# Moving the tiles of a four-layer fp32r kernel in SBUF: three unused pad tiles and a smaller DMA scratch

## The chip, the cores and the metric

The kernel runs on one core of one Trainium2 chip. The metric is the device time of one execution in microseconds (us), lower is better. Times of the kernel before: 1810.0 us, the median of three runs (1809.1 to 1810.69).

## What is computed

`x` holds 2048 positions of 640 features in fp32. Four layers follow one another, A, B, A, B, each `x = x + layer(layernorm(x))` (below, the layer inputs are normalised):

```python
# layer A: 32 heads of 20, each position attends to itself and to 7 earlier ones, 2 apart
q, k, v = split(x @ wqkv)                       # wqkv is 640 x 1920
attn = softmax(q . k[pos - 2*w] * 20**-0.5)     # w = 0..7, masked where pos - 2*w < 0
y = concat_heads(sum_w attn * v[pos - 2*w]) @ wo
# layer B: real part of a 2-D Fourier transform, as matrix products
a, b = x @ dft_hid_re.T, x @ dft_hid_im.T       # 640 x 640
y = dft_seq_re @ a - dft_seq_im @ b             # 2048 x 2048
```

## The kernel before

**Numbers in two parts.** TensorE works on fp32r operands. Every matrix is split into a high part and a low remainder, and each product is three matmuls, high·high, high·low and low·high (`PASSES`). A split tile has the shape `[128, 2, ...]`, with the parts side by side. Nearly all of TensorE's work is of that kind, 8798 matmuls in all, each with its own weight load.

**Layer A** (`layer_a`) goes over 32 units of work (a block of 512 positions and a group of four heads) in steps, and a plan written out in the code gives each step its phases on all engines. `qkv_mm` (L347, matmul at L357) makes the QKV projection of one of 4 position blocks, one of 4 head groups `q` and one of 4 sub-blocks `j`: 15 matmuls of 480 columns, with the transposed input in tile `s{j}` as weights (stationary) and the projection's split weights in tile `r1_{q}` as the moving operand. There are 64 such groups in each layer A. `tp` and the functions `pc_pe` and `pc_sub` transpose 128x128 blocks with the moving operand `ident` (L322) and subtract with the weights `nident` (L330). `wo_mm` (L504) is the output projection. VectorE and GpSimd do the attention itself in tiles `pr0` to `pr3` (L426, L434, L464, L479).

**Layer B** (`LayerB`) has three kinds of matmuls. `z_mm` (L903, matmul at L914) multiplies a normalised input block (`xn[c]`, tile `r1_{c}`, stationary, 128 columns `k`) with a split block of the sequence matrix (`ct[s]`, 512 columns, moving). There are 16 steps `s` of 15 matmuls for one column block: `s // 4` is `c`. The first column block is done inside the end of layer A, with `ct[s]` in tile `s3`, `s0`, `s2` in turn (four tiles in turn from step 12), the second by `run` (L1225) through `zpart` with `ct[s]` in `s3` for even `s` and `s0` for odd `s`. The five banks `m0, m1, xt, t0, t1` take the five `k` of each of the three passes.

The other six column blocks are made in three calls of `pair` (L1089) per layer, with Strassen's scheme of seven products. `product` (L1078, matmul at L1081) issues three matmuls of 512 columns for each of its banks: the weights are 128-column pieces of a tile `r1_c`, the moving operand a split block in `r1_2`, `r1_3`, `s0` or `s1`. A call of `pair` has three sections of eight rounds `i`:

- first, per round, `m5` (six matmuls, banks `m`), `m4` (six, banks `xt` and `t`) and `m7` (six, banks `t` and `pq`): 144 in all. `m4`'s weights lie in `r1_2` and `r1_3`; those of `m5` and `m7` in `r1_0` for rounds 0, 1, 4 and 5, in `r1_1` for the others (`x_slot` goes round a ring of eight places, four in each tile, two places a round).
- second, `m2` (six), `f1` (three), `f2` (three), `m1` (six), `f1` (three): 168 in all. `m1` and `m2` go by the same ring; the first `f1` has `r1_0` for rounds 0 to 3 and then `r1_1`; the others have `r1_2` and `r1_3`.
- third, `m3` (six), `f2` (three), `m6` (six): 120 in all. `m3` and `f2` have `r1_0` for rounds 0 to 3 and then `r1_1`; `m6` has `r1_1`. From round 3 on a twelve-matmul piece of `ymm` stands between the rounds, so that rounds 0 to 3 are one stretch of 60.

Counted over a call, 48 + 60 + 36 = 144 of the 432 matmuls take their weights from `r1_0`. Two layers with three calls make 864 of 2592.

`ymm` (L981, matmul at L992) is the hidden transform: for each of five `k`, twelve matmuls of 320 columns, whose moving operand is in turn `wr` (tile `r2a`) and `wi[k]` (tiles `pr0` to `pr3` and `zo3`), 16 output tiles in each layer.

**Order of the work.** Layer A is written out for all engines. In layer B only TensorE's order is (`tc.manual_schedule`); the order of the other engines and of the loads, which SP issues, is made by the planner of `tile.TileContext(nc, schedule_with_timeline_sim=True)`. The kernel's DMAs are issued from SP, eight of them from ScalarE, none from GpSimd.

**Where a tile lies.** `T` asks the pool for a tile by a tag. A tag gets its place at its first request, in order of the requests, as large as its largest tile and rounded up to 32 bytes per partition; later tiles of the tag use it again. Ahead of them lie the reserved scratch for DMA descriptors (16384 bytes at address 0 when nothing else is asked for) and four constants of 32 bytes. So `warm` begins at 16512. The places that matter, in bytes per partition, with the remainder of the address by 128:

```
warm   16512   0      r1_0  22784   0      pr1   65984  64     r1_3  147904  64
ident  16544  32      pr0   43264   0      r1_1  81344  64     zo2   168384  64
nident 17056  32      win   48384   0,64   r2a  101824  64     s0    185536  64
s3     17568  32      (5 buffers, in turn) r1_2 127424  64     zo0   216512  64
```

The other tiles of matmul operands (`pr2`, `pr3`, `zo1`, `zo3`, `ot`, `s1`, `s2`, `stg`, `xa`) have the remainder 64. The pieces of them that matmuls use begin at multiples of 128 bytes within their tile (480 x 4 = 1920, 320 x 4 = 1280, 128 x 4 = 512), so that a piece has its tile's remainder. The last tile ends at 229312.

Of the kernel before, what the change touches and what calls it, by code (L numbers as in the profile page):

```python
# [26 lines left out]
P = 128  # L27
# [47 lines left out]
def tile_layers(ctx: ExitStack, tc: tile.TileContext, x, wqkv, wo, cs, wre, wim, out):  # L75
    nc = tc.nc
# [9 lines left out]
    def nm(base):  # L86
        uid[0] += 1
        return f"{base}_{uid[0]}"

    def T(shape, tag, dt=F32, bufs=1, pool=None):  # L90
        return (pool or sb).tile(shape, dt, tag=tag, name=nm(tag), bufs=bufs)
# [4 lines left out]
    warm = T([P, 1], "warm")  # L96
    nc.vector.memset(warm, 0.0)
    nc.scalar.activation(warm, warm, AF.Exp)
    ident = T([P, P], "ident")
    make_identity(nc, ident)  # L100
    nident = T([P, P], "nident", F32R)
# [6 lines left out]
    mhalf = T([P, 4], "mhalf")  # L108
    nc.gpsimd.memset(mhalf, -0.5)
    mask = T([P, SLOTS], "mask")  # L110
    nc.gpsimd.memset(mask, 0.0)
    nc.gpsimd.memset(mask[0:2, 0:3], NEG)
    nc.gpsimd.memset(mask[0:1, 3:7], NEG)
# [74 lines left out]
    def load_x(src, j, tag="xa"):  # L188
        xt = T([P, D], tag, bufs={"xa": 2}.get(tag, 1))
        nc.sync.dma_start(xt, src[:, j, :])  # L190
        return xt
# [10 lines left out]
    def wq_load1(q, k):  # L202
        raw = wtile([P, 3 * F])
        nc.sync.dma_start(raw, wqkv[q][:, k, :])
        return raw
# [31 lines left out]
    def layer_a(li, stats, handoff, prev):  # L237
# [21 lines left out]
        def at(step, phase, fn, *args):  # L259
            plan.setdefault((step, phase), []).append((fn, args))  # L260
# [5 lines left out]
        def x_load(c, j, tag="xa"):  # L266
            xnT[(c, j)] = load_x(xin[c], j, tag)

        def x_stats(c, j, fast=False):
            if j == 0:  # L270
                stats[c] = Stats()
            stats[c].tile(j, xnT[(c, j)], fast)

        def x_fin(c, j):
            stats[c].finish(j, j + 1)

        def x_norm(c, j, fast=False):
            stats[c].apply(j, xnT[(c, j)], fast)

        def xt_pe(c, j, part, bank):  # L280
            if part == 0:
                xnT[(c, j, 1)] = T([P, 2, KD, P], f"s{j}", F32R)
            xnT[(c, j, "p", part)] = t_pe(xnT[(c, j)], part, bank)

        def xt_hi(c, j, part):
            t_hi(xnT[(c, j, 1)], part, xnT[(c, j, "p", part)])

        def xt_lo(c, j, part):
            t_lo(xnT[(c, j, 1)], part, xnT[(c, j, "p", part)])
# [236 lines left out]
        def wq_begin(q):  # L526
            wq[q] = T([P, 2, KD, 3 * F], f"r1_{q}", F32R)

        def wq_raw(q):
            if q < 3:  # L530
                if q == 1:
                    wq["raw"] = T([P, 2, KD, 3 * F], "r2a")
                nc.sync.dma_start(wq["raw"][:, q - 1], wqkv[q])
                for k in range(KD):
                    wq[(q, k)] = wq["raw"][:, q - 1, k]
                return
            for i, tag in enumerate(("zo2", "zo3", "ot")):
                k0, k1 = 2 * i, min(2 * i + 2, KD)
                raw = wq_load(q, k0, k1, tag)
                for k in range(k0, k1):  # L540
                    wq[(q, k)] = raw[:, k - k0]
# [64 lines left out]
        def prologue_first():  # L606
            wq_begin(0)
            for j, (k0, k1) in enumerate(((0, 3), (3, 5))):
                x_load(0, j, f"pr{j}")
                for k in range(k0, k1):  # L610
                    wq[(0, k)] = wq_load1(0, k)
            for j in range(2, NJ):
                x_load(0, j, f"pr{j}")
            for q in (1, 2, 3):
                wq_begin(q)
                wq_raw(q)
            w0 = wq[0]

            def whi(k, eng):
                (eng.tensor_copy if eng is nc.vector else eng.copy)(w0[:, 0, k], wq[(0, k)])  # L620

            def wlo(k, eng):
                eng.tensor_tensor(w0[:, 1, k], wq[(0, k)], w0[:, 0, k].bitcast(F32), op=ALU.subtract)

            def xt_all(j, bank):
                return [(xt_pe, (0, j, i, f"{bank}{i}")) for i in range(2)] + [
                    (f, (0, j, i)) for i in range(2) for f in (xt_hi, xt_lo)
                ]

            x_stats(0, 0, True)  # L630
            x_fin(0, 0)
            for k in range(3):
                whi(k, nc.scalar)
            wlo(0, nc.vector)
            x_norm(0, 0, True)
            wlo(1, nc.gpsimd)
            for i in range(2):
                xt_pe(0, 0, i, f"t{i}")
            for i in range(2):
                xt_hi(0, 0, i)  # L640
            x_stats(0, 1, True)
            wlo(2, nc.gpsimd)
            x_fin(0, 1)
            whi(3, nc.vector)
            whi(4, nc.vector)
            for i in range(2):
                xt_lo(0, 0, i)
            wlo(3, nc.vector)
            wlo(4, nc.vector)
            x_norm(0, 1, True)  # L650
            x_stats(0, 2, True)
            x_fin(0, 2)
            mid[0] = xt_all(1, "aux") + [(x_stats, (0, 3, True)), (x_fin, (0, 3)), (x_norm, (0, 2, True))]
            mid[1] = xt_all(2, "t") + [(x_norm, (0, 3, True)), (zero_rows, ())]
            mid[2] = xt_all(3, "aux")
            for i in range(KD):
                at(LEAD0[0] + 1 + i // 2, "misc", wq_split, 1, i)
                at(LEAD0[0] + 3 + i, "misc", wq_split, 2, i)
                at(LEAD0[0] + 5 + i, "misc", wq_split, 3, i)
# [31 lines left out]
        while len(gs) < NGRP:  # L691
            if st % 2 == 0 and len(tx) < NC * NJ:
                c, j = divmod(len(tx), NJ)
# [114 lines left out]
        with tc.manual_schedule(engines=ENGINES):  # L808
            if first:
                prologue_first()  # L810
            nc.vector.tensor_copy(mk, mask)
            for s in range(LEAD0[0], last + 1):
                for ph in PHASES:
                    for fn, args in plan.pop((s, ph), ()):
                        fn(*args)
            pc_pe(67)
            pc_hi(67)
            pc_lo(67, True)
            wo_mm(c, 2, None, 0, 2, 3)
            wo_mm(c, 3, ("pq", "aux0"))  # L820
            wo_add(c, 2)
            wo_stats(c, 2)
            wo_fin(c, 2, 3)
            if first:
                handoff.c_hl(14)
            handoff.ln_tail(c, 2, xr, nstats)
            wo_add(c, 3)
            handoff.ln_lo(c, 2)
            handoff.z_mm(14, None)
            wo_stats(c, 3)  # L830
            wo_fin(c, 3, 4)
            if first:
                handoff.c_hl(15)
            handoff.ln_tail(c, 3, xr, nstats)
            handoff.ln_lo(c, 3)
            handoff.z_mm(15, None)
# [478 lines left out]
```

## Time and profile before

| what | value |
|---|---|
| median of three runs | 1810.0 us (1809.1 to 1810.69) |
| span of the profiled execution, first to last instruction | 1804.2 us |
| mean granted TensorE clock over the span | 0.993 |
| TensorE matmul, busy | 1745.8 us (97%) |
| VectorE, busy | 1392.7 us (77%) |
| ScalarE, busy | 818.3 us (45%) |
| GpSimd, busy | 633.5 us (35%) |

For the profiled execution the profile gives the span alone and no device time of its own; the median of the runs is 5.8 us above that span. A row of the timeline has the start in us from the span's start, the length from the first start to the last end in us, the engine, the line, the operation, the tiles as `output<-inputs` without their buffer numbers (so `r` is any of `r1_0` to `r1_3`, and `s` any of `s0` to `s3`), the shape and the count of instructions that were merged into the row. The end of a matmul is modelled and overlaps the next one, so the pace of a run of matmuls is read from starts alone: start of a later row less start of an earlier one, divided by the matmuls between them. A row of the table by stretches has the stretch, its length, then busy time and count for PE (matmul), PEld (weight load), DVE (VectorE), ACT (ScalarE) and POOL (GpSimd), the granted TensorE clock as a share of full speed, the mean busy share of the DMA engines, and GB/s.

### The profile page before, as it was taken

To read this page: it belongs to the slowest core of one execution; us is meant where nothing else is said; L and a number is where in the kernel's file an instruction comes from. 1 tells how busy PE (TensorE), PEld (TensorE's weight loads), DVE (VectorE), ACT (ScalarE), POOL (GpSimd) and SP (SyncE) were. 2 spreads that over 40 slices of the span, in tenths; PEclk is the share of its full clock that TensorE was granted. 3 is DMA by queue.
4 is the path that set the end of the run, shared out by engine and by line. 5 is a ranking of instruction groups with operands and counts; after the bars stand their busy time and mean duration, and the time that the engine had idled before them with its cause. 6 is when DMAs were issued, how large, how long until landed. Compare 5 with 4: busy or idle time off the path is not lost.

```text
span 1804.2 us, 26493 instructions
## 1 busy us (share of the span) xinstructions
PE 1745.8 (97%) x8798; PEld 1506.7 (84%) x8798; DVE 1392.7 (77%) x2135; ACT 818.3 (45%) x1708; POOL 633.5 (35%) x591
## 2 busy tenths in 40 slices
PE   9999997988999999999999999999899999999999
PEld 7879886877888888888888888888788888888888
DVE  5899899887767767768739988899777677677673
ACT  5544644544445445445633334444434443443441
POOL 3799898960000000000008987889400000000000
PEclk9999999999999999999999999999999999999999
DMA  6776667648777887888737856687687767776761
GB/s 233 224 264 206 208 206 250 211 150 293 255 261 247 293 267 248 290 269 267 251 124 227 278 184 198 201 299 260 218 295 262 262 223 228 264 232 229 254 209 52
DMA packets 273994, 423.59 MB, mean 235 GB/s; under 512 B 22688, under 2 KB 153248, under 8 KB 273600
## 3 DMA queue, kind: packets, MB, share of 16 engines
q1 hardware_dynamic: 270656, 419.92, 70.1%
q10 hardware_dynamic: 3200, 1.97, 0.4%
q8 instruction: 70, 1.15, 0.3%
q14 instruction: 68, 0.56, 0.1%
HBM read 336.66 MB, written 85.14 MB: 234 GB/s over the span
## 4 chain that ended last, share of the span: by engine, by line
PE 64%; DVE 15%; DMA 9%; POOL 6%; issue 3%; ACT 3%; SPq 0%; DVEq 0%; ACTq 0%; POOLq 0%
PE m L357 15%; PE aux L992 12%; PE t L1081 10%; PE m L1081 10%; PE pq L1081 5%; PE xt L1081 5%; PE aux L504 4%; DMA xc<-stg 4%; DVE pr L426 3%; DVE pr L464 2%; POOL pr L479 2%; DMA win<-cs_in 1%; POOL pr L428 1%; DVE lg L434 1%; POOL r L864 1%
## 5 line engine op out<-in xcount | busy, mean ns | idle before, releaser
L357 PE MATMUL m<-r,s 128*128 128x480 f32 x1920 | 438.8, 383 | 7.4 <-ACT s L227 3.5
L357 PEld LDWEIGHTS m<-r,s 128*128 128x128 f32 x1920 | 356.1, 189 | 63.5 <-ACT s L227 5.1
L1074 ACT CAST r<-win 128x512 fp32r<-128x512 f32 x251 | 153.0, 620 | 171.8 <-DVE win L1110 73.1
L169 POOL TENSOR_TENSOR stats<-stats,mhalf 128x1 f32<-128x1 f32 (+1 forms) x40 | 29.1, 727 | 566.3 <-ACT stats L165 566.2
L992 PE MATMUL aux<-r2a,zo 128*128 128x320 f32 x768 | 226.4, 310 | 0.0
L479 POOL TENSOR_TENSOR pr<-pr 128x640 f32<-128x640 f32 x126 | 203.5, 1615 | 43.1 <-DVE pr L464 42.1
L426 DVE TENSOR_TENSOR pr<-pq,win 128x1280 f32<-128x1280 f32 x128 | 189.8, 1483 | 26.7 <-ACT pq L399 26.5
L992 PE MATMUL aux<-pr,zo 128*128 128x320 f32 x704 | 208.2, 308 | 0.0
L1075 DVE TENSOR_TENSOR r<-win,r 128x512 fp32r<-128x512 f32 x251 | 169.2, 687 | 48.2 <-ACT r L1074 45.2
L464 DVE TENSOR_TENSOR pr<-pq,win 128x1280 f32<-128x1280 f32 x128 | 190.8, 1491 | 4.5 <-DVE pq L459 0.2
L428 POOL TENSOR_TENSOR pr<-pr 128x640 f32<-128x640 f32 x128 | 183.7, 1435 | 20.2 <-DVE pr L426 17.2
L1081 PE MATMUL m<-r,r 128*128 128x512 f32 x594 | 153.2, 392 | 0.5 <-ACT r L1074 0.3
L992 PEld LDWEIGHTS aux<-r2a,zo 128*128 128x128 f32 x768 | 144.1, 188 | 2.0
L914 PE MATMUL m<-s,r 128*128 128x512 f32 x384 | 121.8, 404 | 17.2 <-DMA s<-c0b 8.9
L1081 PE MATMUL t<-r,r 128*128 128x512 f32 x495 | 134.0, 392 | 0.0
L992 PEld LDWEIGHTS aux<-pr,zo 128*128 128x128 f32 x704 | 132.2, 188 | 2.0
L1081 PEld LDWEIGHTS m<-r,r 128*128 128x128 f32 x594 | 111.2, 188 | 26.1 <-DVE r L1075 0.9
L914 PE MATMUL t<-s,r 128*128 128x512 f32 x384 | 119.0, 398 | 2.4 <-DVE ot L974 2.4
L480 POOL TENSOR_TENSOR pr<-pr 128x320 f32<-128x320 f32 x126 | 114.8, 911 | 9.9
L364 ACT COPY stg<-m 128x480 f32<-128x480 f32 x128 | 70.8, 555 | 98.8 <-PE m L357 87.1
L434 DVE TENSOR_REDUCE lg<-pr 128x64 f32<-128x640 f32 x128 | 103.9, 812 | 11.3 <-POOL pr L428 11.0
L1081 PEld LDWEIGHTS t<-r,r 128*128 128x128 f32 x495 | 93.0, 188 | 21.3
(270 smaller groups left out, 3239.6 us busy)
## 6 DMA issues: line engine op xcount, KB each, us to landing
win<-cs_in SPq DMA_DIRECT2D x358, 256.0 KB, 4.2
r<-xc SPq DMA_DIRECT2D x240, 256.0 KB, 4.4
win<-kvb SPq DMA_DIRECT2D x96, 440.0 KB, 4.9
xa<-cs_in SPq DMA_DIRECT2D x124, 256.0 KB, 4.0
win<-kvb SPq DMA_DIRECT2D x64, 360.0 KB, 4.8
xc<-stg SPq DMA_DIRECT2D x40, 512.0 KB, 3.5
kvb<-stg SPq DMA_DIRECT2D x60, 320.0 KB, 3.8
xr<-xs SPq DMA_DIRECT2D x40, 320.0 KB, 3.1
```

The source lines that it names most:

```text
L357: nc.tensor.matmul(mt[g][:, : 3 * F], st[:, a, k], wq[q][:, b, k], start=n == 0, stop=n == 14)
L426: nc.vector.tensor_tensor(pr, q, wview(u, jp, 0, [[1, FE]]), op=ALU.mult)
L428: nc.gpsimd.tensor_tensor(pv[:, :, 0:10], pv[:, :, 0:10], pv[:, :, 10:20], op=ALU.add)
L434: nc.vector.tensor_reduce(lgs[u][:, 2 * jp : 2 * jp + 2].rearrange("p j w h -> p (j w h)"), prq.pop((u, jp))[:, :, 0:10], axis=AX.X, op=AL ...
L464: nc.vector.tensor_tensor(pr.rearrange("p j w (h d) -> p j w h d", d=DH), lgs[u][:, 2 * jp : 2 * jp + 2].unsqueeze(4).to_broadcast([P, 2, ...
L479: g.tensor_tensor(pr[:, :, 0:4], pr[:, :, 0:4], pr[:, :, 4:8], op=ALU.add)
L480: g.tensor_tensor(pr[:, :, 0:2], pr[:, :, 0:2], pr[:, :, 2:4], op=ALU.add)
L914: self.last = nc.tensor.matmul(self.z[t][k], self.xn[c][:, a, j, k * P : (k + 1) * P], self.ct[s][:, b], start=s == 0 and i == 0, stop=s = ...
L992: self.last = nc.tensor.matmul(self.ym[e][:, :320], zt[(k, a, ri)][:, j2 * P : (j2 + 1) * P], w[:, e * 320 : (e + 1) * 320], start=(k, a, ...
L1074: nc.scalar.copy(hi, raw)
L1075: nc.vector.tensor_tensor(lo, raw, hi.bitcast(F32), op=ALU.subtract)
L1081: nc.tensor.matmul(bank, w(a, kb), hl[b], start=start and (a, b) == (0, 0), stop=stop and (a, b) == (1, 0),)
```

## The change

```diff
     nc.scalar.activation(warm, warm, AF.Exp)
+    T([P, 8], "pad0")
     ident = T([P, P], "ident")
...
     mask = T([P, SLOTS], "mask")
+    T([P, 40], "pad1")
     nc.gpsimd.memset(mask, 0.0)
...
             for j, (k0, k1) in enumerate(((0, 3), (3, 5))):
+                if j:
+                    T([P, 16], "pad2")
                 x_load(0, j, f"pr{j}")
...
-    nc = bacc.Bacc("TRN2", target_bir_lowering=False, num_devices=1)
+    nc = bacc.Bacc("TRN2", target_bir_lowering=False, num_devices=1, dynamic_dma_scratch_size=1024)
```

Three tiles of 32, 160 and 64 bytes per partition are asked for and never written or read, and the reserved scratch shrinks from 16384 to 1024 bytes. No instruction is added, removed or changed. By the rule above the tiles now lie so (worked out by hand from the sizes):

```
warm    1152   0      r1_0   7616  64      pr1   50880  64     r1_3  132800  64
ident   1216  64      pr0   28096  64      r1_1  66240  64     zo2   153280  64
nident  1728  64      win   33216  64,0    r2a   86720  64     s0    170432  64
s3      2240  64      (5 buffers, in turn) r1_2 112320  64     zo0   201408  64
```

`ident`, `nident` and `s3` go from remainder 32 to 64, `r1_0` and `pr0` from 0 to 64, and the buffers of `win`, which no matmul reads, swap 0 and 64. Everything from `pr1` on moves down by 15104 bytes, 118 times 128, and keeps its remainder.

## Prediction

> **What bounds the kernel now.** I read the page first: the span, the busy times and the shares of the chain, then the queues.
>
> ```profile
> span 1804.2 us, 26493 instructions
> PE 1745.8 (97%) x8798; PEld 1506.7 (84%) x8798; DVE 1392.7 (77%) x2135; ACT 818.3 (45%) x1708; POOL 633.5 (35%) x591
> ...
> q1 hardware_dynamic: 270656, 419.92, 70.1%
> q10 hardware_dynamic: 3200, 1.97, 0.4%
> ...
> PE 64%; DVE 15%; DMA 9%; POOL 6%; issue 3%; ACT 3%; SPq 0%; DVEq 0%; ACTq 0%; POOLq 0%
> ```
>
> TensorE is busy for 97% of the span and has 64% of the chain that ended last. Because a busy matmul is not a matmul at its peak, I then asked for the table by stretches, to see where TensorE never stops.
>
> ```profile
> 120.00:250.00 130.00, 130.00 (x688) 116.15 (x687) 117.73 (x169) 68.69 (x181) 117.78 (x114) 1.00 0.66 207
> 250.00:430.00 180.00, 157.81 (x797) 134.43 (x796) 159.04 (x235) 87.10 (x199) 133.64 (x119) 0.96 0.67 217
> 430.00:490.00 60.00, 59.08 (x295) 50.66 (x294) 45.45 (x70) 24.07 (x44) 0.00 (x0) 1.00 0.79 284
> 490.00:890.00 400.00, 397.00 (x1958) 339.05 (x1957) 294.68 (x480) 199.67 (x370) 5.21 (x6) 1.00 0.79 265
> ...
> 1370.00:1804.00 434.00, 430.32 (x2187) 374.35 (x2185) 294.48 (x484) 174.71 (x302) 0.00 (x0) 1.00 0.66 219
> ```
>
> The last two rows are the calls of `pair`: TensorE is occupied for 397.00 of 400 us and 430.32 of 434, VectorE for 74% and 68%. In `run` (430 to 490) it is 59.08 of 60. Only the end of layer A (250 to 430) leaves TensorE open, for 22 us. In layer B, then, the pace of the matmuls is the time, and the question is whether that pace depends on where an operand begins. The timeline of one first section of `pair`, TensorE alone, answers it.
>
> ```profile
> 636.27 0.84 PE L1081 MATMUL xt<-r,r 128*128 128x512 f32 x3
> ...
> 643.07 1.56 PE L1081 MATMUL m<-r,r 128*128 128x512 f32 x6
> ...
> 651.45 1.55 PE L1081 MATMUL m<-r,r 128*128 128x512 f32 x6
> 652.83 0.39 PE L1081 MATMUL xt<-r 128*128 128x512 f32 x1
> ```
>
> The six matmuls `m` are `m5` of rounds 4 (at 643.07) and 6 (at 651.45). Before 643.07 come rounds 2 and 3, whose weights from the ring lie in `r1_1` (remainder 64); from 643.07 to 651.45 come rounds 4 and 5, with `r1_0` (remainder 0). From 636.27 to 643.07 there are 30 matmuls in 6.80 us, 226.7 ns each. From 643.07 to 651.45 there are 36 in 8.38 us, 232.8 ns each. Shape, moving tiles, DMA traffic and clock (1.00 in this stretch) are alike. Moreover 12 of these 36 are `m4` products, whose weights lie in `r1_3`: the slow tile drags its neighbours along. The first six matmuls after the return to `r1_1` still take 1.38 us (651.45 to 652.83) where six clean ones take 1.36.
>
> The same comparison for a moving operand is in `run`, where the sequence matrix lies in `s3` and `s0` by turns:
>
> ```profile
> 452.05 0.63 PE L914 MATMUL m<-s,r 128*128 128x512 f32 x2
> ...
> 455.55 0.62 PE L914 MATMUL m<-s,r 128*128 128x512 f32 x2
> ...
> 458.95 0.63 PE L914 MATMUL m<-s,r 128*128 128x512 f32 x2
> ```
>
> The step from 452.05 (`s3`, remainder 32) takes 3.50 us for 15 matmuls, the step from 455.55 (`s0`, remainder 64) 3.40 us, with weights in `r1_2` both times. So 233.3 against 226.7 ns again, from the other operand. I choose this reading: a 512-column matmul whose operands both begin at remainder 64 takes 226.7 ns, and about 6.6 ns more if either does not. Whether 64 itself counts, or that both have the same remainder, the trace can't tell; after the change both hold for every matmul.
>
> **The change part by part.** It removes and adds no instruction, wait or DMA, so no queue (SP's and GpSimd's among them) is passed by a moved step, and no wait is added. The smaller scratch costs nothing: the kernel's traffic is on hardware queues (q1: 270656 packets, against 3200 on q10, which is hardware too), and no DMA is issued from GpSimd. What remains is the pace at new addresses, term by term.
>
> *`pair`, L1081.* The second and third sections show the size:
>
> ```profile
> 1690.56 0.86 PE L1081 MATMUL xt<-s,r 128*128 128x512 f32 x3
> ...
> 1729.21 0.30 PE L992 MATMUL aux<-r2a,zo 128*128 128x320 f32 x1
> ...
> 1738.03 0.86 PE L1081 MATMUL xt<-r,r 128*128 128x512 f32 x3
> ...
> 1751.93 0.30 PE L992 MATMUL aux<-r2a,zo 128*128 128x320 f32 x1
> ```
>
> The second section has 168 matmuls from 1690.56 to 1729.21: 38.65 us, against 168 x 0.2267 = 38.08, so 0.57 us too many. The stretch of 60 in the third takes 13.90 us from 1738.03 to 1751.93, against 13.60: 0.30. For the first section, rounds 2 to 5 (636.27 to 651.45, 66 matmuls in 15.18 us, 230.0 each) give 144 x 3.3 ns = 0.48. Together 1.35 us per call, less 0.02 for each of three stretches that will still begin with a few slow matmuls after `ymm`: 1.29. Six calls: **7.7 us**. TensorE waits for nothing here that would take the gain back: in the stretch from 490 to 890 the longest waits are these two,
>
> ```profile
> PE t L1081 <- DVE ot L974: 1.1, 1, 1.1
> PE xt L1081 <- DVE r L1075: 1.0, 1, 1.0
> ```
>
> and VectorE has a quarter of the time free. If that cover were gone, half of the term is a fair price (second rival).
>
> *`run`, second column block of `z_mm`.* Ten of 16 steps have an operand off 64 (0 to 3 by `r1_0`, 4, 6, 8, 10, 12 and 14 by `s3`): 10 x 0.10 us x 2 layers = **2.0 us**, on the path by 59.08 of 60.
>
> *First column block, inside layer A.* Seven of 16 steps (0 to 3, 6, 9, 12): 1.4 us for both layers. TensorE waits for others in this stretch, so some of it turns into longer waits. Bounds 0 and 1.4; I take half, **0.7**.
>
> *QKV, L357, 480 columns.* Groups with `r1_0` and groups with clean tiles:
>
> ```profile
> 131.38 6.75 PE L357 MATMUL m<-r,s 128*128 128x480 f32 x30
> 137.97 0.60 PE L322 MATMUL xt<-ident,xa 128*128 128x128 f32 x4
> ...
> 142.92 3.38 PE L357 MATMUL m<-r,s 128*128 128x480 f32 x15
> 146.14 0.60 PE L322 MATMUL xt<-ident,xa 128*128 128x128 f32 x4
> ...
> 180.28 3.42 PE L357 MATMUL m<-r,s 128*128 128x480 f32 x15
> 183.54 0.60 PE L322 MATMUL xt<-ident,xa 128*128 128x128 f32 x4
> ```
>
> Two groups of `r1_0` take 6.59 us (131.38 to 137.97), 219.7 ns per matmul; a group of `r1_1` with `s1` 3.22 us (142.92 to 146.14), 214.7; a group of `r1_3` with `s1` 3.26 us (180.28 to 183.54), 217.3. The gain is thus 2.4 to 5 ns here, and scatter among clean groups is as large, so that nothing is possible too. Off 64 are 16 groups of `q` = 0 and 12 others with `s3` per layer: 56 x 15 = 840 matmuls. At 2 ns, near the lower rows, that is 1.7 us, bounds 0 and 4.2. In 120 to 250 TensorE is never idle, earlier and later it is; I count 70%: **1.2 us**.
>
> *`ymm`, L992, 320 columns, first `k` with `pr0`.*
>
> ```profile
> 1730.99 0.31 PE L992 MATMUL aux<-r2a,zo 128*128 128x320 f32 x1
> ...
> 1732.75 0.31 PE L992 MATMUL aux<-r2a,zo 128*128 128x320 f32 x1
> ```
>
> The twelve with `pr0` (1729.21 to 1730.99) take 1.78 us, the next twelve with `pr1` 1.76: 0.02 x 32 output tiles = **0.6 us**, bounds 0 and 0.6.
>
> *Transposes with `ident` and `nident`*: some 430 small matmuls; at most 6 ns each gives 0 to 2.6; as they are short, **0.1**.
>
> *The other engines* read and write the moved tiles too:
>
> ```profile
> L426 DVE TENSOR_TENSOR pr<-pq,win x128: 1474/1483/1493, 33.9 to 1266.7; 128x1280 f32<-128x1280 f32 x128
> L1075 DVE TENSOR_TENSOR r<-win,r x251: 677/685/694, 467.6 to 1761.2; 128x512 fp32r<-128x512 f32 x126
> ```
>
> These are least, median and longest durations in ns. L426 writes `pr0` (remainder 0) and `pr2` (64) by turns and reads `win` at both remainders, and all 128 lie within 19 ns; L1075 reads `win` at both within 17 ns. So VectorE's cost is nothing, within 1%.
>
> The sum: 7.7 + 2.0 + 0.7 + 1.2 + 0.6 + 0.1 = 12.3 us off a span of 1804.2, which leaves 1791.9. The runs' median lies 5.8 us above the span; 1791.9 + 5.8 = **1797.7 us**. With the lower bounds (7.7, half of 2.0, nothing else) 8.7 us and 1801.3; with the upper ones (7.7, 2.0, 1.4, 4.2, 0.6, 2.6) 18.5 us, though TensorE waits in most of the stretches that hold the last terms, so I end at 16.5: 1793.5.
>
> **The rivals.**
>
> *The address isn't the cause: 1810 us.* `s3` and `r1_0` are also the two lowest-lying of the large operand tiles (17568 and 22784), and after the change they lie lower still. If it is the place in memory, or some use that the two tiles share, nothing moves. Against it: one is slow as moving operand and the other as weights, at two remainders, while the tiles at 64, from `r1_1` at 81344 upward, keep the clean pace. For it: no tile at remainder 64 lies low, so that the trace can't part the two. The Trainium skill, "SBUF — State Buffer", section "Specifications (TRN2)", gives lines of 16 bytes; starts at 0, 32 and 64 all lie at a line's start, so by that rule this change brings nothing. The Trainium skill, "TensorE: Matmul & The Clock Gate", section "Wait — 56ns, not 53.3ns?", gives warm back-to-back matmuls a pace from their columns and the clock alone, 215.7 ns at 512, which would be no change either; the trace's 226.7 and 232.8 at the same width agree with neither that figure nor with one pace.
>
> *Something else becomes the bound: 1804 us.* With TensorE 1.3% faster in `pair` (1.29 us of 98), loads and VectorE's sums (DMA share 0.79, VectorE 74%) may come late in places. Half of the forecast's gain, 6 us, would remain: 1804. For it: the two waits of about 1 us above. Against it: both shares leave room, and TensorE hardly ever waited.
>
> *More time at half clock, and slower: 1818 us.* Where TensorE waits for long in layer A its granted clock falls afterwards:
>
> ```profile
> 1202.00:1205.40 3.40, 3.40 (x11) 2.54 (x10) 3.33 (x5) 0.00 (x0) 3.17 (x5) 0.50 1.01 390
> ...
> PE m L914 <- DMA s<-c0b: 8.9, 4, 2.8
> ```
>
> In these 3.4 us the clock was 0.50, after a wait of the kind in the second row (8.9 us in four, the longest 2.8). Such a stretch costs about 1.7 us of work. Faster matmuls reach those waits earlier and so wait longer; every wait that grows to about 2.8 us adds a stretch. The change is slower from ten more stretches on (12.3 / 1.7 is 7.2 for no change, 3.6 us more makes 9.4); twelve make 1797.7 + 20.4 = 1818. Against it: there are few waits near that length, and the gain lies in layer B, where there are none. One or two stretches more or fewer are likely, and move the forecast by 3 us.
>
> **How the numbers follow.** Forecast as summed, 1793.5 to 1801.5: 0.71. Half of it, to 1805: 0.16. Nothing: 0.08. Slower by the clock: 0.04. Better than 1793.5: 0.01. About 0.2%, 3.6 us, is what a measurement of this kernel can tell from no change: faster means below 1806.4. So 0.71 + 0.16 + 0.01 = 0.88 faster, 0.08 the same, 0.04 slower. The range holds the first two cases: 1793.5 to 1805.
>
> **What would show it right or wrong.** Right: a second section of `pair` in 38.1 us instead of 38.65; steps of `run` all at 3.40; the 60 in 13.6; VectorE's durations as they are. Wrong: a section that still takes 38.65 us (first rival); 38.1 us with new waits around it (second); more stretches at clock 0.50 in layer A (third). If `r1_0` and `r1_1` now run alike but at 233 ns, a low place or the common remainder was the matter.

## The result and the profile after

| | before | after |
|---|---|---|
| median of six runs, us | 1810.35 (1809.1 to 1816.39) | 1803.6 (1801.87 to 1807.75) |
| span of the profiled execution, us | 1804.2 | 1800.0 |
| its device time, us | not given | 1801.87 |
| its mean granted clock | 0.993 | 0.991 |

The ratio of the times is 0.9961, with a 95% interval of 0.9945 to 0.9976: 7 us faster (4.3 to 10), or 0.39%. The order of the instructions on every engine is the one of before. The device time of the changed kernel's profiled execution lies 1.8 us above its span, and so it does in the experiments that give both (1809.6 and 1807.8 in scratch_only). So before's profiled execution took about 1806.0, 4 us less than the median of its runs, and the two profiles, 4.2 us apart, understate the change. The page of the changed kernel, busy times and shares of the chain that ended last:

```profile
span 1800.0 us, 26493 instructions
PE 1735.3 (96%) x8798; PEld 1506.4 (84%) x8798; DVE 1391.0 (77%) x2135; ACT 818.6 (45%) x1708; POOL 633.5 (35%) x591
...
PE 63%; DVE 14%; DMA 11%; POOL 6%; ACT 3%; issue 2%; SPq 0%; DVEq 0%; ACTq 0%; POOLq 0%
```

TensorE's busy time falls by 10.5 us (1745.8 to 1735.3), that of VectorE by 1.7, but the span by 4.2 only. In the chain, TensorE and VectorE have a point less each and DMA two more (9% to 11%). The pace itself is what was forecast. The timeline of TensorE in the changed kernel, the same second and third section as in the prediction, and a piece of the first section of which it showed the slow rounds (line numbers are four higher):

```profile
641.26 1.52 PE L1085 MATMUL m<-r,r 128*128 128x512 f32 x6
...
649.42 1.52 PE L1085 MATMUL m<-r,r 128*128 128x512 f32 x6
...
1687.22 0.39 PE L1085 MATMUL xt<-s,r 128*128 128x512 f32 x1
...
1725.32 0.30 PE L996 MATMUL aux<-r2a,zo 128*128 128x320 f32 x1
...
1734.12 0.86 PE L1085 MATMUL xt<-r,r 128*128 128x512 f32 x3
...
1747.74 0.30 PE L996 MATMUL aux<-r2a,zo 128*128 128x320 f32 x1
```

Rounds 4 and 5 (36 matmuls, 641.26 to 649.42) take 8.16 us, 226.7 ns each, where they took 232.8. The second section (168) takes 38.10 us, where it took 38.65. The 60 of the third take 13.62, where they took 13.90. But the table by stretches shows something else beside it:

```profile
430.00:490.00 60.00, 58.11 (x284) 48.73 (x283) 44.59 (x70) 24.17 (x44) 0.00 (x0) 1.00 0.78 275
490.00:890.00 400.00, 396.31 (x1968) 340.82 (x1969) 296.06 (x484) 201.74 (x374) 5.23 (x6) 1.00 0.81 266
1370.00:1800.00 430.00, 425.00 (x2181) 372.97 (x2179) 292.85 (x483) 173.90 (x302) 0.00 (x0) 1.00 0.68 220
```

From 430 to 490, mostly `run`, TensorE is busy for 58.11 us where it was for 59.08: part of the time saved on the matmuls is open time now. (The counts, 284 against 295, can't be compared, since the stretch no longer begins and ends at the same matmuls.)

**Where the 12 us went.** To separate the two I took the starts of all 8798 matmuls. The time from one start to the next counts as pace up to a cap (242 ns at 512 columns, 226 at 480, 160 at 320), what is beyond as waiting; work lost in stretches at half clock is kept apart. The differences in pace hold within 1 us however the caps are set; between the last two rows 1 to 2 us go over with another cap. In us, for the kernel before, the one after and four of the experiments below:

| | before | scratch_only | after | only_r1 | slow_run | far128 |
|---|---|---|---|---|---|---|
| pace | 1710.7 | 1710.7 | 1698.4 | 1702.5 | 1703.0 | 1707.1 |
| waiting | 79.5 | 81.6 | 86.3 | 84.1 | 81.9 | 84.2 |
| lost at half clock | 9.3 | 10.7 | 10.5 | 9.7 | 12.4 | 10.8 |

The changed kernel saves 12.3 us of pace and gives 6.8 back in waits and 1.2 at half clock. Against scratch_only, which has the pace of the kernel before and a profile nearer to its median, it gives back 4.7 in waits and hardly anything at half clock.

### The profile page after: what moved, and what is told of

It is laid out like the page before. It is cut to its first block, busy times and chain, and to the rows that moved or that the text cites. A ratio compares the mean times of both kernels' runs of the same rounds, so it can differ in the third digit from the quotient of the medians.

```text
span 1800.0 us, 26493 instructions
## 1 busy us (share of the span) xinstructions
PE 1735.3 (96%) x8798; PEld 1506.4 (84%) x8798; DVE 1391.0 (77%) x2135; ACT 818.6 (45%) x1708; POOL 633.5 (35%) x591
## 4 chain that ended last, share of the span: by engine, by line
PE 63%; DVE 14%; DMA 11%; POOL 6%; ACT 3%; issue 2%; SPq 0%; DVEq 0%; ACTq 0%; POOLq 0%
PE m L359 16%; PE aux L996 12%; PE t L1085 9%; PE m L1085 9%; PE pq L1085 5%; PE xt L1085 4%; DMA xc<-stg 4%; PE aux L506 4%; DVE pr L428 2%; DMA win<-cs_in 2%; DVE pr L466 2%; POOL pr L481 2%; POOL pr L430 1%; POOL r L868 1%; DMA xa<-cs_in 1%
```

## The experiments

Two questions were open. First, what sets the pace: the place in memory (the first rival; scratch_only), the remainder 64 itself (theory 1 of the expectations), or that both operands have the same remainder. Second, why only about half of the pace arrived.

### scratch_only: the smaller scratch, no pads

```diff
-    nc = bacc.Bacc("TRN2", target_bir_lowering=False, num_devices=1)
+    nc = bacc.Bacc("TRN2", target_bir_lowering=False, num_devices=1, dynamic_dma_scratch_size=1024)
```

> Only the scratch shrinks; every tile moves down by 15360 bytes (120 x 128) and keeps its remainder. Theory 1 (a 512-column matmul runs at 226.7 ns only if both its operands begin at remainder 64): the second section of pair stays at 38.65 us, the steps of run with s3 at 3.50 us, time as before within 2 us (1808 to 1812). Theory 2 (what both operands need is the same remainder): the same as theory 1 here. Theory 3 (the low place of s3 and r1_0, or the scratch itself): pair's sections and the time move, toward the 1803.6 us of the changed kernel if the scratch did it.

Measured: 1809.98 us, ratio 0.9991 (0.9978 to 1.0005). The timeline, TensorE, second section:

```profile
1694.16 0.39 PE L1081 MATMUL xt<-s,r 128*128 128x512 f32 x1
...
1732.81 0.30 PE L992 MATMUL aux<-r2a,zo 128*128 128x320 f32 x1
```

It takes 38.65 us, as before. All tiles lie 15360 bytes lower and nothing changes, so that neither the low place in memory nor the smaller scratch is the cause.

### only_r1, only_s3: half of the change each

All with the small scratch. `only_r1` leaves out `pad0`, so that `r1_0` and `pr0` come to 64 and `ident`, `nident`, `s3` stay at 32. `only_s3` brings `ident`, `nident`, `s3` to 64 and leaves `r1_0` and `pr0` at 0.

```diff
# only_r1
+    T([P, 16], "pad1")
...
+                if j:
+                    T([P, 16], "pad2")
# only_s3
+    T([P, 8], "pad0")
...
+    T([P, 24], "pad1")
```

> r1_0 and pr0 go to remainder 64, ident, nident and s3 stay at 32. Theories 1 and 2: all of pair at 226.8 ns per matmul (second section 38.1 us), which is 7.4 us less TensorE work in the six calls; the steps of run with s3 stay at 3.50 us. About 3 us of the gain is lost to stages in which TensorE isn't the bound, as in the changed kernel: 1804 to 1806. If the loss of the changed kernel comes from run and its s3 steps, the same time as the changed kernel.

> ident, nident and s3 go to remainder 64, r1_0 and pr0 stay at 0. Theories 1 and 2: pair stays at 230 ns (second section 38.65 us), steps of run with s3 and weights in r1_1 to r1_3 go to 3.40 us, 1.2 us less TensorE work in run and 0.6 in layer A. If run is paced by the stores of x_combine (two buffers stg), none of the 1.2 us shows: 1808 to 1811. If TensorE paces run: 1807 to 1809.

Measured: `only_r1` 1802.62 us, ratio 0.9951 (0.9931 to 0.997); `only_s3` 1809.24, ratio 0.9997 (0.9982 to 1.0012). The timeline of `only_r1`, second section:

```profile
1688.31 0.39 PE L1084 MATMUL xt<-s,r 128*128 128x512 f32 x1
...
1726.41 0.30 PE L995 MATMUL aux<-r2a,zo 128*128 128x320 f32 x1
```

That is 38.10 us. The weights' half alone gives all that the whole change gives. The other half gives nothing, and its steps in `s3` had not even become clean: 233.0 ns, though the tile has remainder 64 like its weights. Neither theory 1 nor "the same remainder by 128" explains that. For the same reason `only_s3` doesn't answer the second question of its expectation, whether faster steps in `run` would show: they weren't faster.

### all0: every operand at remainder 0

Again with the small scratch.

```diff
+    T([P, 24], "pad0")
...
+    T([P, 8], "pad1")
...
+                if j:
+                    T([P, 16], "pad2")
```

> All operands of matmuls begin at remainder 0. Theory 1 (64 itself counts): no matmul is at its best, pair at 233.3 ns throughout (second section 39.2 us), about 9 us more TensorE work in pair and 3 in z_mm than before: 1815 to 1822. Theory 2 (the same remainder counts): pair at 226.8 ns (38.1 us) as in the changed kernel, 1802 to 1806. Theory 3 (low place): as before, 1810.

Measured: 1803.37 us, ratio 0.996 (0.9945 to 0.9975). The timeline, second section:

```profile
1688.82 0.39 PE L1085 MATMUL xt<-s,r 128*128 128x512 f32 x1
...
1726.92 0.30 PE L996 MATMUL aux<-r2a,zo 128*128 128x320 f32 x1
```

38.10 us at remainder 0, so it isn't 64 that counts, but what the two operands have in common. Theory 1 falls. The steps in `s3` stayed slow here too (233.1 ns). By 256, `s3` begins at 0 and the other operands at 128.

### offsets: one operand moved in steps of some bytes

In `run` the moving operand of steps 4 to 14 begins 4, 8, 16, 24, 32, 48, 64, 80, 96, 112 and 128 bytes later in its tile; the rest is the changed kernel.

```diff
-            self.ct[s] = T([P, 2, 512], tag, F32R)
+            if t:
+                o = (0, 0, 0, 0, 1, 2, 4, 6, 8, 12, 16, 20, 24, 28, 32, 0)[s]
+                wide = T([P, 1056], tag, F32R)
+                self.ct[s] = wide[:, o : o + 1024].rearrange("p (a t) -> p a t", a=2)
+            else:
+                self.ct[s] = T([P, 2, 512], tag, F32R)
```

> The changed kernel, with the sequence-matrix tile of run's steps 4 to 14 begun 4, 8, 16, 24, 32, 48, 64, 80, 96, 112 and 128 bytes after remainder 64; weights stay at 64. Theory 2a (both operands must have the same remainder by 128): only steps up to 3 and the steps at 128 and 0 run at 226.7 ns in their steady part, all the others at about 233. Theory 2b (only a 32-byte or larger part of the address counts): the steps at 4, 8, 16 and 24 run at 226.7 too. Theory 2c (the price grows with the distance): 228 near, 233 far.

Measured: 1802.98 us, from a single run. The timeline of TensorE; rows that start a step of 15 matmuls, moved by 4, 8, 16 and, from 474.42, by 128 bytes:

```profile
435.74 0.62 PE L923 MATMUL m<-s,r 128*128 128x512 f32 x2
...
439.29 0.62 PE L923 MATMUL m<-s,r 128*128 128x512 f32 x2
...
442.78 0.63 PE L923 MATMUL m<-s,r 128*128 128x512 f32 x2
...
446.26 0.63 PE L923 MATMUL m<-s,r 128*128 128x512 f32 x2
...
474.42 0.62 PE L923 MATMUL m<-s,r 128*128 128x512 f32 x2
...
477.90 1.54 PE L923 MATMUL m<-s,r 128*128 128x512 f32 x6
```

At 4 bytes a step takes 3.55 us, at 8 3.49, at 16 3.48 and at 128 3.48, where a clean one takes 3.40. Of the matmuls that follow at least six like themselves without a wait (some 16 for each distance over both layers, four at 112), the mean ns:

| distance, bytes | 0 | 4 | 8 | 16 | 24 | 32 | 48 | 64 | 80 | 96 | 112 | 128 |
|---|---|---|---|---|---|---|---|---|---|---|---|---|
| ns | 226.9 | 238.1 | 234.1 | 231.7 | 234.1 | 233.3 | 231.6 | 228.6 | 231.2 | 233.8 | 227.2 | 232.8 |

A distance of 128 bytes is slow, while pieces that are 256 bytes or a multiple apart are fast in every kernel here. The theory that I formed from this (theory 4): a 512-column matmul has the clean pace where its operands' addresses **agree by 256 bytes**. The other direction, that no other distance has it, isn't shown: at 64 the price is under 2 ns, and at 112 the last nine matmuls of the first layer's step ran at 226 to 227 ns, while the second layer's step, broken by waits, never settled. It explains `only_s3` and `all0`, where `s3` is 128 bytes by 256 away from its weights, and the change itself, after which all operand tiles have the remainder 192 by 256. The Trainium skill, "SBUF — State Buffer", section "Specifications (TRN2)", has lines of 16 bytes. If these lines alone counted, 16, 32 and 48 would do as well as 0; 231.6 to 233.3 ns against 226.9 say otherwise.

### far128: all at 64 by 128, but 128 apart

```diff
-                    T([P, 16], "pad2")
+                    T([P, 48], "pad2")
```

On the changed kernel. Every operand still lies 64 bytes past a multiple of 128, as the change is described, but `r1_0`, `s3` and the identities are 128 bytes off the rest by 256.

> The changed kernel with 128 more bytes in pad2: every operand still begins 64 bytes past a multiple of 128, but r1_0, s3 and the identities now lie 128 bytes (by 256) away from r1_1 to r1_3, s0 to s2 and the rest. Theory 4 (moving operand and weights must agree by 256 bytes): r1_0's products in pair are slow again, the second section takes 38.6 us, steps of run with s3 are slow in their steady part, time as before, 1808 to 1811. Theory 2a (agreement by 128): second section 38.1 us, time as the changed kernel, 1802 to 1805.

Measured: 1808.69 us, ratio 0.9986 (0.9975 to 0.9996). The timeline, second section:

```profile
1693.34 0.39 PE L1085 MATMUL xt<-s,r 128*128 128x512 f32 x1
...
1731.92 0.30 PE L996 MATMUL aux<-r2a,zo 128*128 128x320 f32 x1
```

38.58 us, the slow pace again, with 233.1 ns for the products with `r1_0`, at distance 128. So 64 past a multiple of 128 isn't the condition, and agreement by 128 isn't enough; agreement by 256 is.

### pitch512: does it hold for the QKV projection?

There the split weights' rows are 480 elements, 1920 bytes, so that every second one is 128 bytes off by 256. Here the rows are padded to 512 elements.

```diff
-        wt = T([P, 2, KD, 3 * F], f"r1_{q}", F32R)
+        wt = T([P, 2, KD, 512], f"r1_{q}", F32R)[:, :, :, : 3 * F]
...
-            wq[q] = T([P, 2, KD, 3 * F], f"r1_{q}", F32R)
+            wq[q] = T([P, 2, KD, 512], f"r1_{q}", F32R)[:, :, :, : 3 * F]
```

> The changed kernel with the QKV weights' rows 512 elements apart in place of 480 (the tile's place is large enough already). A piece then begins at a multiple of 256 bytes from the next, where 896 of the 1920 QKV matmuls of the changed kernel lie 128 bytes away from their weights. Theory 4: L357's matmuls go from 216.1 ns in the mean to about 213.5, 5 us less TensorE work in layer A. If layer A hands on as much of it as it did of the change's 1.8 us there (about a third to two thirds): 1800 to 1802.5. Theory 2a: no change, 1802 to 1805.

Measured: 1803.83 us, ratio 0.9966 (0.9956 to 0.9977), so no faster than the changed kernel. A matmul of 480 columns takes 216.9 ns where it takes 216.1 in the changed kernel; the forecast for agreement was 213.5. In the changed kernel itself the matmuls whose operands agree by 256 take 216.6 ns, those at 128 take 215.5. The theory doesn't hold at 480 columns, and why is open.

### slow_run: is `run` paced by TensorE?

All 16 steps of `run` get the worst distance, 4 bytes; the rest is the changed kernel.

```diff
-            self.ct[s] = T([P, 2, 512], tag, F32R)
+            if t:
+                self.ct[s] = T([P, 1032], tag, F32R)[:, 1:1025].rearrange("p (a t) -> p a t", a=2)
+            else:
+                self.ct[s] = T([P, 2, 512], tag, F32R)
```

> The changed kernel with the sequence-matrix tile of all 16 steps of run begun 4 bytes off, where a matmul took 238 ns: about 11 ns for each of 480 matmuls, 4.5 to 5.3 us more TensorE work than in the changed kernel. Theory A (run is paced by the stores of x_combine, so that TensorE's pace there doesn't count): under 1.5 us slower than the changed kernel, 1802.5 to 1805. Theory C (TensorE paces run): all of it shows, 1808 to 1809.

Measured: 1802.36 us, ratio 0.9955 (0.9943 to 0.9967), no slower than the changed kernel, though 480 matmuls take 237.3 ns instead of 226.9, which is 5 us. By the starts, `run` itself, up to the first matmul of `pair`, does get longer in the two layers, from 76.1 and 76.2 us to 77.3 and 76.6. The first section behind it makes that up: 33.6 and 33.3 us where it takes 34.8 in both layers of the changed kernel. So TensorE's pace in `run` counts for nothing from the end of that section on. The waits from 428 to 486, in the kernel before, the changed one and `slow_run`, in this order (engine, line and tile that wait, for whom; us in all, times, longest):

```profile
ACT stg L1046 <- DVE stg L1045: 24.6, 13, 4.5
DVE stg L1045 <- DMA xc<-stg: 9.3, 7, 3.2
ACT s L886 <- PE t L914: 6.5, 4, 2.4
```

```profile
ACT stg L1050 <- DVE stg L1049: 28.6, 16, 3.7
DVE stg L1049 <- DMA xc<-stg: 9.7, 7, 3.2
...
ACT s L890 <- PE t L918: 2.5, 3, 1.3
```

```profile
ACT stg L1053 <- DVE stg L1052: 21.4, 12, 3.3
DVE stg L1052 <- DMA xc<-stg: 8.2, 7, 2.8
ACT s L893 <- PE t L921: 8.2, 5, 2.4
```

With faster matmuls ScalarE's wait for TensorE falls from 6.5 to 2.5 us, and its wait in `x_combine`, for VectorE's part of `stg`, grows by the same 4.0; with slower ones it is 8.2 and 21.4. By the trace, what paces `run` is another chain: `x_combine` writes the sums into `stg`, of which there are two buffers, and VectorE waits until the stores of the last ones have landed. The chain of waits from 425 to 480, by line, says so, in the kernel before, the changed one and `slow_run`:

```profile
by line: DMA xc<-stg 64.3%; DVE stg L1045 10.9%; DVE s L1037 9.6%; DVE stg L1047 9.4%; issue 5.0%; DVE r L1075 3.0%; DVE s L899 2.4%; ACT stg L1046 2.3%; DVE zo L128 1.0%; DVEq L1045 0.1%; ACTq L1046 0.0%
```

```profile
by line: DMA xc<-stg 54.6%; DVE stg L1049 12.1%; DVE stg L1051 10.5%; DVE s L1041 9.9%; issue 3.8%; ACT stg L1050 3.4%; DVE r L1079 3.0%; DVE s L903 2.3%; DVE zo L130 0.8%; ACTq L1050 0.1%; DVEq L1049 0.0%
```

```profile
by line: DMA xc<-stg 41.1%; DMA xa<-wim_in 9.3%; DVE s L1044 8.3%; PE t L921 7.8%; PE m L921 7.8%; DVE stg L1052 7.2%; DVE stg L1054 5.1%; issue 5.0%; PE xt L921 3.9%; DVE r L1082 3.0%; PE aux L999 2.9%; DVE zo L130 1.5%; DVE s L906 1.4%; D
```

No matmul is in the first two, in a stretch in which TensorE is busy for 58 to 59 of 60 us. In `slow_run` those of L921 come in with 19.5%: TensorE and the stores are then about level, and the time is still no longer. The shares vary between executions (scratch_only, with the pace of before, has the stores at 37.2% and L914 at 5.1%; far128 has 31.3% and, for the same matmuls, 19.0%), but the stores lead in all of them. That TensorE doesn't pace `run` is what `slow_run` shows; that the stores do is read from the chain, since no run here shortens them alone.

### after_stg4, base_stg4, after_win9, pool_stg4: more room for the stores

If two buffers of `stg` are the limit, four should let the gain through. `after_stg4` is the changed kernel with four, `base_stg4` scratch_only with four. `after_win9` has nine buffers of `win` for five. `pool_stg4` moves the sum of `x_whole` and the first sum of `x_combine` from VectorE to GpSimd as well.

```diff
# after_stg4, base_stg4, and the same in the other four places of stg
-            hl = T([P, 2, 2, 256], "stg", F32R, bufs=2)
+            hl = T([P, 2, 2, 256], "stg", F32R, bufs=4)
# pool_stg4, besides
-            nc.vector.tensor_tensor(self.whole[side], v[:, 0], v[:, 1], op=ALU.add)
+            nc.gpsimd.tensor_tensor(self.whole[side], v[:, 0], v[:, 1], op=ALU.add)
...
-            nc.vector.tensor_tensor(lo.bitcast(F32), va, vb, op=op)
+            nc.gpsimd.tensor_tensor(lo.bitcast(F32), va, vb, op=op)
```

> The changed kernel with four buffers of stg in place of two, in the room that the smaller scratch left. Theory A (the missing half of the gain was lost in run, where x_combine's stores hold its two buffers, and at the sections' borders): run gets shorter by the 1 us per layer that the matmuls saved and by waits, 1798 to 1801. Theory B (the loss is scatter of the half-clock stretches and of waits in layer A): as the changed kernel, 1802 to 1805.

> Four buffers of stg at the remainders of before (scratch 1024, no pads). Theory A: run isn't held by the stores, so it is paced by its slower matmuls: 1808 to 1810, and the distance to the changed kernel with four buffers grows from 6.7 to 9 or 10 us. Theory B: 1810, distance 6 to 7 us.

> The changed kernel with nine buffers of win in place of five. If the new waits in layer B (first sum of a round waiting for its loads) come from loads that start late because win is full, they go, about 2 us: 1800 to 1802. If they come from VectorE and ScalarE, as their order says, or from the queue, no change: 1802 to 1805. A new order by the planner can move it either way.

> The changed kernel with four buffers of stg, and the sums of x_whole and the first sum of x_combine on GpSimd, which is idle in run, in place of VectorE. If what holds the end of run is VectorE's queue (the evacuation of the second column block stands behind sums that wait for buffers), the evacuation comes earlier and the first section of the first call of pair loses its long waits: section 33 us in place of 34.8, 1798 to 1802. If the four buffers by themselves make the planner place run's work badly, as in the kernel with four buffers alone, it stays near 1815. In between, both count.

Measured, in this order: 1814.84 us, ratio 1.0025 (1.0012 to 1.0038); 1822.19, ratio 1.0069 (1.0047 to 1.0091; a fourth run, of 3470 us, is left out of the ratio); 1810.49, ratio 1.0001 (0.9985 to 1.0017); 1831.65, ratio 1.0111 (1.0093 to 1.0128). All four missed what was expected. With other buffers the planner makes another order for the engines and the loads, and TensorE's waits grow. Over the whole span, TensorE's longest waits in `after_stg4`, then in `pool_stg4`:

```profile
PE aux L996 <- ACT zo L128: 9.6, 2, 5.3
```

```profile
PE m L918 <- DVE s L903: 17.6, 6, 7.2
```

In the changed kernel the longest are these two:

```profile
PE m L918 <- DMA s<-c0b: 7.1, 4, 2.5
PE aux L506 <- DVE xa L156: 6.5, 2, 4.4
```

The waits of 9.6 and 17.6 us are new. So these kernels don't test whether the stores are the limit; they change too much beside it. The pair of `stg` runs tells one thing: between the two, both with four buffers, the change is worth 7.4 us (1822.19 less 1814.84), no more than with two. The 9 us or more that the first theory expected with four buffers did not come.

## Why the prediction was right in its course, and forecast nearly twice the gain

It stayed in its range, with the sign right and the pace of the matmuls as the cause. But the favoured case, 1793.5 to 1801.5 with a chance of 0.71, did not come: 12.3 us came out as 7. 1803.6 lies in the range only because the range took in the second rival as well. Point by point:

**The pace: right.** By the starts of all matmuls, the products gained 7.4 us (forecast 7.7), both column blocks of `z_mm` 2.3 (3.4 before the first block was halved for its waits), QKV 1.8 (1.7 before the 70%), `ymm` 0.3 (0.6), transposes at most 0.3 (0.1). Without these discounts the forecast's pace adds up to 13.5; that the 12.3 of pace equals the 12.3 of the forecast, from which part had been taken off for waits, is chance. VectorE's two rows of the prediction are within 1 ns of before, and its total on the page within 0.2%.

**First rival, the address isn't the cause: fell.** scratch_only and far128 show it from both sides. What the prediction left open, 64 or a common remainder by 128, is neither: agreement by 256 bytes gives the clean pace. In the layout of before the tiles with remainder 64 by 128 happen to agree by 256, so that the trace couldn't part the two. That the three pads brought agreement by 256 too was luck: far128 has remainder 64 for every operand, which is all that the prediction asked for, and its second section stays slow (38.58 us).

**The step that failed: "on the path by 59.08 of 60".** The term of `run`, 2.0 us, was counted whole because TensorE was occupied, and the first column block and QKV in part. To see where the gain arrived I lined up ten profiles of the same order, matmul by matmul, four with slow products (before, scratch_only, only_s3, far128) and six with fast ones (after, only_r1, all0, offsets, slow_run, pitch512). The mean length of each stretch in us:

| stretch | slow products | fast products | difference |
|---|---|---|---|
| up to `run`, first layer A | 409.2 | 409.4 | +0.1 |
| `run` and the first call's first section | 110.7 | 110.5 | -0.2 |
| the rest of the first layer B's products | 366.3 | 364.2 | -2.1 |
| up to the second layer's `run` | 415.8 | 415.9 | +0.1 |
| `run` and the first call's first section | 110.6 | 111.0 | +0.3 |
| the rest of the second layer B's products | 360.0 | 357.2 | -2.8 |

All of the gain that these profiles show lies where `pair` runs behind the first call's first section. `run` and that section together aren't shortened by a faster TensorE, which reaches earlier there what isn't ready yet. In layer A nothing shows either, but kernels of one group lie 2 to 4 us apart there, so that a gain of 1 us could hide. Whole runs say the same: `slow_run` (0.9955 for 0.9961) has 4.6 us more pace than the changed kernel, `only_r1` (0.9951), whose steps in `s3` stay slow, has 4.1 us more, and neither is slower. So of the terms 2.0, 0.7 and 1.2 nothing is seen in the time, nor of the first calls' first sections, 0.5 per layer. The row that pointed at `run` was in sight: `xc<-stg` with 4% of the page's chain, and in this stretch 64.3%. The profiles show less than the runs: the ten spans differ by 4.6 us between the groups (1805.5 to 1800.9), the medians of the runs by some 6.5, and where the other 2 us lie isn't known.

**"TensorE waits for nothing here that would take the gain back": half wrong.** In the second layer B four of the six fast kernels pass on 3.2 to 3.4 us of the 3.4 that is left to the products after the first section (3 x 1.29 less 0.48); `slow_run` and pitch512 pass on 2.0 and 1.6. In the first layer B, on average, 2.1 arrive. TensorE's waits from 490 to 890 in the changed kernel:

```profile
PE t L1085 <- DVE ot L978: 1.9, 1, 1.9
PE xt L1085 <- DVE r L1079: 0.7, 2, 0.4
```

The wait at the start of the first call grew from 1.1 us to 1.9; it is the first section's, which the table has. Which waits take the other 1.3 us of the first layer B isn't settled: the chain passes through the stores of `c0b` near 585 us, but no run took them away.

**Second rival, something else becomes the bound, half of the gain remains, 1804: this is what happened**, with a chance of 0.16. Its mechanism was loads and VectorE's sums in `pair`; what showed is `run`, whose chain leads through the stores, and only the 1.3 us of the first layer B may be lost in the way that the rival named.

**Third rival, half clock: not shown.** The changed kernel has 30.7 us at half clock against 23.9, nine stretches of 3.4 against seven, but the kernels with fast products range from 20.5 us to 37.5, and scratch_only, with no change in pace, has 27.3. Nor was 2.8 us the length of wait that adds a stretch: in the kernel before one of 2.3 us is followed by one and one of 2.5 us isn't, and in the changed kernel one of 1.8 us is.

## What to carry to other kernels

Before a faster instruction is counted as time, look at the chain of waits in that stretch, not at the engine's busy share: matmuls that are pipelined fill 59 of 60 us and still wait for something else. A stretch is paced by an engine if slowing that engine there costs time; giving its operands a slow distance is a cheap and clean test, which changes neither order nor buffers, whereas more buffers made the planner write another program. Read its answer in the time of the whole kernel: `slow_run` made `run` up to 1.2 us longer, and the next section took it back. Where fp32r matmuls of 512 columns matter, let the moving operand and the weights agree by 256 bytes, and compare addresses by more than the first power of two that fits.

## What the runs showed of the hardware

- The pace of a 512-column fp32r matmul with a weight load of its own depends on the distance of its two operands by 256 bytes: 226.7 ns at 0, 228.6 at 64, 231 to 234 at most others, 238.1 at 4, and 227.2 at 112, from four matmuls only. It didn't depend on the place of either: all tiles 15360 bytes lower left the second section at 38.65 us, and the common remainders 64, 128 and 192 by 256 all gave 38.10.
- The Trainium skill, "TensorE: Matmul & The Clock Gate", section "Wait — 56ns, not 53.3ns?", gives 215.7 ns for warm back-to-back matmuls of 512 columns. No steady stretch of 512-column fp32r matmuls in these kernels reached it; their best is 226.7.
- At 320 columns the dependence is small: the twelve matmuls of a group's first `k`, half of which read `pr0`, took 147.6 ns each in the kernel before, where `pr0` lay 64 bytes off, and 146.3 after; the others took about 146.5 in both. At 480 columns the mean was 217.0 ns before, 216.1 after, and agreement by 256 was no better than a distance of 128.
- After a wait or a run of `ymm` some five matmuls are slow (228 to 236 ns) before the pace is clean, and in `pair` the six behind the products of a slow tile are too (1.38 us for 1.36), so that a slow tile costs its neighbours. In `run` the step behind a slow one has just one slow matmul.
